# TensorE's order of matmul sets from a literal list in place of greedy rules, with 26 more score tiles on VectorE

## The chip, the core and the metric

The kernel runs on one NeuronCore of a Trainium2 chip. Times are device microseconds from start to end of one execution. Executions of one kernel mostly agree within 0.4%. In the profile PE is TensorE, PEld its weight loads, ACT ScalarE, DVE VectorE, POOL GpSimd.

## The reference

Two branches over the same input of 2048 rows of 512, mixed by a gate: attention with 32 heads of 16, and a gated MLP of width 1792.

```python
x = A_x
g = sigmoid((x * gate_w).sum(-1, keepdims=True))
a = softmax(q @ k.T * 16**-0.5) @ v ... @ wo          # 32 heads, 2048 x 2048 scores each
b = (sigmoid(x @ w_gate) * (x @ w_up)) @ w_down
return g * a + (1 - g) * b
```

The scores are the bulk: 32 units (8 groups of four heads by 4 chunks of 512 queries) of 64 tiles of 128 x 512, so 2048 tiles, each of which has to be exponentiated and multiplied with the values.

## The kernel before

The program is made by a scheduler that runs when the kernel is built. It holds tasks with assumed durations, walks through modelled time, and writes down an order for every engine. On the chip each engine plays its list, with semaphore waits where a task needs another engine's result or a buffer that another engine still uses. Nothing is chosen at run time.

A score tile goes one of two ways. Most ("R" tasks) are read from PSUM by ScalarE, two or three at a time, and written as exp into `PA`. Some ("RD") are read by VectorE, which forms exp from an integer conversion into a half-precision bit pattern and two shifted copies of it, so that such a tile needs three products with the values in place of one. How many go there is set by unit, in pairs:

```python
D_HALVES = (9, 9, 8, 8, 10, 6, 10, 9, 8, ...)     # pairs of tiles on VectorE, by unit

def make_exp(ts):                                  # ScalarE: 1, 2 or 3 tiles
    e = P.add("act", 0.175 + 0.3665 * len(ts), lambda a: a.activation(some(PA, out), some(ps_all, bs), ACTF.Exp, ...))
def make_x(ds):                                    # VectorE: conversion; two phase copies follow
    return P.add("dve", 0.076 + 0.534 * len(ds), lambda v: v.tensor_scalar(PDu[...], some(ps_all, bs), EXP_A, EXP_B, ...))
```

TensorE works in sets. A score set holds one to four score matmuls, each on its own quarter of the array's rows ("R" mode); a product set, or one step of a projection or of the MLP, holds four matmuls on quarters of the columns ("C" mode). All eight banks of PSUM, the memory that TensorE writes its results to, are shared by scores, products and projections; a bank is free again when another engine has read it. Which set comes next was decided by rules with some twenty thresholds, each with its own value by unit:

```python
def _pe(self, now):
    k = self.k = KNOBS[min(UNITS - 1, int(self.prog))]
    ...
    if p.nd == 0 and not late_d and nA + 2 <= k.N_A and ps.pick(2):      # scores possible?
        lead = self._lead(now)                                            # work queued on ScalarE
        ...                                                               # two or three tiles, VectorE's if due
        if lead < ((k.LATE_R if due and not ds else k.LATE) if len(s) >= 3 or whole else k.LATE_2) or (whole and lead < k.EARLY):
            return self._issue(s + ds, now, "R", [s + ds])
    ...                                                                   # VectorE's tiles that are behind
    low = ... sum(w for t, w in self.recent if t > now - WINDOW) < WARM
    if low and not hard: ... return self._fill(now)                       # a matmul with zero weights
    ...                                                                   # products, then projections and MLP
```

## Time and profile before

| | before |
|---|---|
| time, median | 748.98 us at first; 750.01 with the run beside the changed kernel |
| span in the profile | 747.7 us |
| busy: PE, ACT, DVE | 736.4, 718.3, 665.1 us |
| ScalarE: first exp, end of last exp | 13.6, 737.7 us |
| ScalarE's work between them, and what it loses | 699.6, 24.5 us |

Busy time is a poor guide: instructions overlap, so an exp that starts late within its predecessor's last 0.25 us leaves no idle time. I price each instruction at the median distance from its start to the next one's where the engine did not idle (0.904 us for an exp of two tiles, 1.330 for three, 0.477 for a tanh); "loss" is what is left of the stretch. (The prediction has 699.7 and 24.4, from a slightly different price for the small ones; its 13.0 of visible idle time includes 1.9 before the first exp.) The lines of the profile are in the prediction.

### The profile page before, as it was taken

How to read it: one execution, taken by the hardware profiler on the slowest of the kernel's cores; microseconds unless marked ns; L12 is line 12 of the kernel's file. 1: busy time of each engine (PE TensorE's matmuls, PEld its weight loads, DVE VectorE, ACT ScalarE, POOL GpSimd, SP SyncE). 2: the span in 40 equal slices, each digit the busy share in tenths (PEclk: the TensorE clock that was granted, in tenths of full speed). 3: DMA queues.
4: the chain of work that ended last, by engine and by line, in shares of the span. 5: the costliest groups of instructions: out<-in, count | busy, mean ns of one | idle time of the engine just before them, and what ended most of it. 6: DMA issues, size and time to landing. Idle time of an engine off the chain costs nothing.

```text
span 747.7 us, 22002 instructions
## 1 busy us (share of the span) xinstructions
PE 736.4 (98%) x9687; PEld 218.3 (29%) x9689; DVE 665.1 (89%) x1277; ACT 718.3 (96%) x790; POOL 149.5 (20%) x279
## 2 busy tenths in 40 slices
PE   9999999999999999999999999999999999999998
PEld 4332422322222222322222222222222222222232
DVE  3999999989988998889999999999996897899985
ACT  4899999999999999999999999999999999999995
POOL 5746456222011030011211000040112000000000
PEclk9999999999999999999999999999999999999999
DMA  8532111132010010101101000010101011000100
GB/s 165 163 85 44 24 23 23 44 79 38 9 23 15 16 37 11 21 15 23 23 16 24 8 23 16 22 37 16 17 16 22 16 23 23 9 9 9 16 2 30
DMA packets 59127, 23.17 MB, mean 31 GB/s; under 512 B 52000, under 2 KB 58008, under 8 KB 59032
## 3 DMA queue, kind: packets, MB, share of 16 engines
q1 hardware_dynamic: 57160, 21.11, 13.1%
q8 instruction: 76, 1.25, 0.7%
q10 hardware_dynamic: 1872, 0.66, 0.4%
q14 instruction: 19, 0.16, 0.1%
HBM read 7.60 MB, written 2.10 MB: 13 GB/s over the span
## 4 chain that ended last, share of the span: by engine, by line
ACT 56%; PE 39%; DVE 4%; SPq 1%; DMA 1%; issue 0%
ACT PA L1000 53%; PE ps_all L798 14%; PE ps_all L1046 13%; PE ps_all L1055 11%; ACT tT L984 3%; DVE PD L1016 1%; DVE PD L1011 1%; SPq L704 1%; DMA xT<-in_A_x_dram 1%; PE ps_all L942 1%; DVE am L859 0%; DVE un L846 0%; DVE V L956 0%; ACT un L832 0%; ACT V L954 0%
## 5 line engine op out<-in xcount | busy, mean ns | idle before, releaser
L1000 ACT ACTIVATE PA<-ps_all 128x1024 bf16<-128x1024 f32 (+1 forms) x720 | 698.8, 1181 | 13.0 <-PE ps_all L1046 8.1
L1016 DVE TENSOR_SCALAR PD<-ps_all 128x512 uint16<-128x512 f32 (+1 forms) x557 | 374.4, 690 | 49.5 <-PE ps_all L1046 40.1
L1046 PE MATMUL ps_all<-Q,K 32*128 32x512 bf16 x2032 | 303.1, 384 | 4.2 <-ACT PA L1000 2.6
L1055 PE MATMUL ps_all<-PA,V 128*17 128x512 bf16 x1486 | 229.0, 381 | 0.4 <-ACT PA L1000 0.2
L1011 DVE TENSOR_SCALAR PD<-PD 128x1024 uint16<-128x1024 uint16 (+1 forms) x490 | 219.6, 475 | 2.1
L1055 PE MATMUL ps_all<-PD,Vm 128*17 128x512 f16 x1124 | 178.9, 381 | 0.0
L1046 PEld LDWEIGHTS ps_all<-Q,K 32*128 32x128 bf16 x2032 | 76.3, 91 | 292.4 <-ACT PA L1000 249.4
L1055 PE MATMUL ps_all<-PD,V 128*17 128x512 f16 x562 | 134.3, 381 | 0.0
L1135 POOL TENSOR_TENSOR rs<-rec,e 128x16 f32<-128x16 f32 x32 | 8.5, 266 | 363.6 <-DVE rec L1133 363.6
L798 PE MATMUL ps_all<-xT,wg 128*32 128x512 bf16 x896 | 71.4, 384 | 0.0
L798 PE MATMUL ps_all<-un,hT 128*32 128x512 bf16 x896 | 70.5, 383 | 0.0
L798 PE MATMUL ps_all<-xT,wu 128*32 128x512 bf16 x896 | 69.1, 383 | 0.0
L1055 PEld LDWEIGHTS ps_all<-PA,V 128*17 128x17 bf16 x1486 | 53.8, 88 | 48.1 <-issue 36.6
L1055 PEld LDWEIGHTS ps_all<-PD,Vm 128*17 128x17 bf16 x1124 | 41.5, 88 | 38.1 <-issue 32.0
L987 DVE SCALAR_TENSOR_TENSOR hT<-tT,ps_all 128x512 bf16<-128x512 bf16 x56 | 38.1, 680 | 8.0 <-PE ps_all L798 7.1
L984 ACT ACTIVATE tT<-ps_all 128x512 bf16<-128x512 f32 x56 | 42.5, 763 | 0.0
L1055 PEld LDWEIGHTS ps_all<-PD,V 128*17 128x17 bf16 x562 | 31.5, 88 | 19.0 <-issue 14.9
L914 POOL COPY Q<-Q 128x512 bf16<-128x512 bf16 x15 | 9.9, 661 | 122.7 <-DVE Q L913 122.6
L817 POOL TENSOR_TENSOR mid<-mid 128x256 bf16<-128x256 bf16 (+3 forms) x60 | 28.4, 473 | 3.7
L798 PEld LDWEIGHTS ps_all<-xT,wu 128*32 128x32 bf16 x896 | 19.2, 95 | 26.8 <-issue 15.2
L798 PEld LDWEIGHTS ps_all<-un,hT 128*32 128x32 bf16 x896 | 18.6, 94 | 24.9 <-issue 17.6
L851 POOL TENSOR_SCALAR K<-un,msk 128x512 bf16<-128x512 bf16 x28 | 24.6, 886 | 2.5 <-ACT un L834 2.3
(106 smaller groups left out, 345.3 us busy)
## 6 DMA issues: line engine op xcount, KB each, us to landing
wg<-in_B_w_gate_dram SPq DMA_DIRECT2D x4, 448.0 KB
wu<-in_B_w_up_dram SPq DMA_DIRECT2D x4, 448.0 KB
un<-in_B_w_down_dram SPq DMA_DIRECT2D x7, 256.0 KB
out_dram<-ost SPq DMA_DIRECT2D x14, 128.0 KB
mid<-mid SPq DMA_TRANSPOSE x60
wo<-in_A_wo_dram SPq DMA_DIRECT2D x2, 256.0 KB
Q<-mid SPq DMA_DIRECT2D x30, 4.0 KB
un<-in_A_wqkv_dram SPq DMA_DIRECT2D x1, 384.0 KB
```

Source lines behind the costliest of these rows:

```text
L798: i = pe.matmul(bk(b)[32 * j:32 * j + 32, :], w()[:, 32 * j:32 * j + 32], x(), start=first, stop=last, tile_position=(0, 32 * j), skip_gro ...
L817: e = pl(0.22 + 0.054 * n, lambda g, n=n: g.tensor_tensor(v()[:, :, 0:n], v()[:, :, 0:n], v()[:, :, n:2 * n], ALU.add), [e], prio=0.5, buf ...
L851: eK[g, r, c] = P.add("pool", 1.0, lambda p, r=r: p.tensor_scalar(K[:, g, r, c * 512:(c + 1) * 512], kraw[:, kr.slot, :], msk[:, r:r + 1], ...
L914: cp = P.add("pool", 0.7, lambda p: p.tensor_copy(Q[:, bq.slot, 1, :], Q[:, bq.slot, 0, :]), [ev], [bq], kind="m")
L984: et = P.add("act", 0.48, lambda a: a.activation(tT[:, t_.slot, :], bk(b), ACTF.Tanh, scale=0.5), [l1], [b, t_], kind="m")
L987: e_h[c, ft] = P.add("dve", 0.62, lambda v: v.scalar_tensor_tensor(hT[:, h_.slot, :], tT[:, t_.slot, :], 1.0, bk(b2), ALU.add, ALU.mult), ...
L1000: e = P.add("act", 0.175 + 0.3665 * len(ts), lambda a: a.activation(some(PA, out), some(ps_all, bs), ACTF.Exp, bias=ACT_BIAS, scale=SCALE) ...
L1011: return v.tensor_scalar(a[:, :, x.n, :], a[:, :, 0, :], float(PH_OFF[x.n]), None, op0=ALU.add)
L1016: return P.add("dve", 0.076 + 0.534 * len(ds), lambda v: v.tensor_scalar(PDu[:, bp.slot, 0, i:i + len(ds), :], some(ps_all, bs), EXP_A, EX ...
L1046: return pe.matmul(bk(b), K[32 * j:32 * j + 32, g, r, kt * 128:(kt + 1) * 128], q, start=True, stop=True, tile_position=(32 * j, 0))
L1055: return pe.matmul(bk(bo_)[32 * j:32 * j + DH + 1, :], lhs(h), rhs(), start=t.first, stop=t.last, tile_position=(0, 32 * j), skip_group_ch ...
L1135: e2_ = P.add("pool", 0.2, lambda p: p.tensor_tensor(r4(rs), r4(rec), e2[:, 4 * c:4 * c + 4][:, :, None].to_broadcast([128, 4, 4]), ALU.mu ...
```

## The change

The intent: replace rules that decide one set at a time by a list found by search, have fewer and fuller score sets, and let VectorE take more of the exps. The scheduler still runs, but PE's part of it reads symbols: `R01.0` is a score set of the first two waiting ScalarE tiles and the first waiting VectorE tile, `C00123` a product set of all four lanes, `G`/`F` the start/next step of a projection or MLP group, `Z` a filler, `w2` "let two chances pass".

```diff
-D_HALVES = (9, 9, 8, 8, 10, 6, 10, 9, 8, 9, 10, 10, 7, ...)     # 562 tiles
+D_HALVES = (9, 9, 9, 9, 10, 7, 10, 10, 9, 10, 10, 10, 8, ...)   # 588 tiles
-LAT = {"pe": 0.25, ...}
+LAT = {"pe": 0.215, ...}
-KNOB_TABLE = dict(N_A=((5, 3), (6, 3), ...), ...)
+ORDER = ("0:F 1:C00123 2:R01.0 3:G 4:R01. 5:R01.1 ...",
+         "M333333333333333N00030003<0000000003000000300003030000000004400000300030=...",   # 2751 sets
+         "0 1 2 3 4 5 6 7 8 9 10 11 12 13 14 15 17 25 29 ...")                              # which group each G is
     def _pe(self, now):
-        k = self.k = KNOBS[min(UNITS - 1, int(self.prog))]
-        ...                                     # all rules
+        if self._next(now):
+            self.passed = 0
+            return True
+        self.passed += 1
+        return False
-        e = P.add("act", 0.175 + 0.3665 * len(ts), ...
+        e = P.add("act", 0.05 + 0.427 * len(ts), ...
-            x = P.add("dve", 0.36, ...
+            x = P.add("dve", 0.334, ...
```
(Cut: the rest of the list, the decoder, and some thirty assumed durations of this kind.)

## The prediction

> **What bounds the kernel now.** I read four views in this order: the page's busy shares and chain, the stretches by stage, the instruction groups by shape, and the chain in order of time. The page first:
>
> ```profile
> PE 736.4 (98%) x9687; PEld 218.3 (29%) x9689; DVE 665.1 (89%) x1277; ACT 718.3 (96%) x790; POOL 149.5 (20%) x279
> ...
> ACT 56%; PE 39%; DVE 4%; SPq 1%; DMA 1%; issue 0%
> ```
>
> Two engines look full, and the chain changes hands between them. ScalarE (ACT) computes exp of most score tiles, VectorE (DVE) of the rest. The stretches (us, then busy time of PE, weight loads, DVE, ACT, POOL) show that this is no average over unlike stages:
>
> ```profile
> 100.00:300.00 200.00, 198.33 (x2609) 56.97 (x2601) 182.43 (x342) 197.19 (x221) 47.98 (x81) 1.00 0.13 30
> 300.00:500.00 200.00, 198.13 (x2385) 54.76 (x2385) 186.93 (x357) 199.33 (x220) 26.94 (x50) 1.00 0.09 20
> 500.00:700.00 200.00, 199.55 (x2561) 55.67 (x2553) 176.64 (x340) 199.41 (x226) 18.50 (x36) 1.00 0.09 16
> ```
>
> For 600 us ACT idles 4 us and PE 4 us, at granted clock 1.00; DVE idles 54 us. Next, the costly groups by shape (count, then busy us and mean ns):
>
> ```profile
> L1000 ACT ACTIVATE PA<-ps_all 128x1024 bf16<-128x1024 f32 x674 | 640.2, 1159 | 6.2 <-PE ps_all L1055 3.4 <-PE ps_all L1046 2.5
> L1016 DVE TENSOR_SCALAR PD<-ps_all 128x512 uint16<-128x512 f32 x552 | 368.3, 685 | 49.4 <-PE ps_all L1046 40.1 <-PE ps_all L1055 4.9
> L1046 PE MATMUL ps_all<-Q,K 32*128 32x512 bf16 x2032 | 303.1, 384 | 4.2 <-ACT PA L1000 2.6
> L1011 DVE TENSOR_SCALAR PD<-PD 128x1024 uint16<-128x1024 uint16 x418 | 171.7, 434 | 2.1
> L1000 ACT ACTIVATE PA<-ps_all 128x1536 bf16<-128x1536 f32 x46 | 69.2, 1505 | 6.9 <-PE ps_all L1046 5.6 <-PE ps_all L1055 0.8
> ```
>
> The mean of an exp over two tiles, 1159 ns, is not its cost: consecutive ones overlap. The spacing is. The chain shows it, start, length, what:
>
> ```profile
> 400.99 38.51 ACT PA L1000 x42
> 439.50 0.05 issue
> 439.54 0.39 PE ps_all L1046 x2
> 439.93 0.32 PE ps_all L1055 x4
> 440.25 0.43 PE ps_all L798 x8
> 440.69 0.33 PE ps_all L1046 x4
> 441.01 0.54 PE ps_all L1055 x8
> ```
>
> 42 exps take 38.51 us, 0.917 each. Start-to-start over the whole trace, the median is 0.904 for two tiles (90th percentile 0.947), 1.330 for three, 0.477 for a tanh. Then the chain passes to PE, where a score set (L1046: up to four matmuls together, one per quarter of the rows) or a set of four column matmuls (L1055, L798) costs about 0.22 us, and 0.32 when the next set is of the other kind.
>
> **ACT's budget.** 674 x 0.904 + 46 x 1.330 + 56 x 0.477 + 2.5 (small ones) = 699.7 us. The first exp starts at 13.6, the last ends at 737.7, and 9.9 us of tail follow (last products, transposes, output projection, store). 747.7 - 13.6 - 9.9 = 724.1, so ACT loses **24.4 us**: 13.0 in the visible idle times, the rest in exps that start some 10 to 100 ns late but within their predecessor's overlap. By stage: about 7 us from 13.6 to 100, where projections crowd PE, 14 from 100 to 700, 3 after.
>
> **PE's budget.** From the first score at 13.2 us, grouping matmuls that start together, spacing is at its floor nearly everywhere: median 221 to 226 ns between sets of one kind, 321 and 322 across a change of kind. All time above the medians sums to **19.3 us**. DVE's instructions, priced at their back-to-back medians (0.601 per score tile, 0.335 per phase copy, 0.599 for two merged), sum to 632.7 us; DVE has room.
>
> **What the Trainium skill says.** "TensorEngine Tiling (Array Packing)", section Key Properties: "Changing tiling mode (not just tile) drains the TensorE". The trace agrees: 322 against 221 ns, some 100 ns a change, 1464 changes. "TensorE: Matmul & The Clock Gate", section Back-to-back issue gap, gives N/2.4 + 2.5 ns for a warm matmul, 216 ns at N = 512; same-kind spacing has its 10th percentile at 216. That figure is for one matmul; the trace shows one set of four in that time, so a half-empty set costs as much as a full one. "ScalarE: Activation LUTs", section What ACT_TABLE_LOAD costs, gives 0.833 ns per element plus 186 ns with immediates, less about 93 of overlap: 946 ns at 1024. The trace has 904, which I use. The clock page's section on HAM oscillation warns of a slower clock after idle windows of some 3.4 us; clock 1.00 throughout here, and that is what the filler matmuls are for.
>
> **The change part by part.** It keeps every operation but the split, and replaces the greedy rules, which chose TensorE's next set from a model when the program was built, by a literal list. The retuned durations affect only the planned order of the other engines and the waits. I decoded the list by counting its symbols, and counted the same in the kernel before's program:
>
> - Score sets: 843 before, 719 after, for the same 2048 tiles (2.43 and 2.85 to a set). Before: 260 sets of two ACT tiles alone and 124 of one DVE tile alone. After: 152 and 33; 538 are two ACT tiles with one DVE tile. That is -124 x 0.2165 = -26.8 us of PE.
> - Probability-times-value sets: 814 to 827. A tile moved to VectorE needs three products in place of one (52 more): +13 x 0.22 = +2.9.
> - Fillers: 10 to 2 (40 such matmuls show in the trace, in tens of sets of four): -8 x 0.22 = -1.7. Projections and MLP: unchanged, 1171.
> - Changes of kind after the first score: 1464 to 1428: -36 x 0.105 = -3.8.
>
> PE's sum: **-29.4 us**. With stalls as before PE alone would give 749.0 - 29.4 = 719.6; without its stalls, about 700.
>
> ACT: 1486 to 1460 tiles, in 692 twos, 25 threes and a single: 625.6 + 33.3 + 0.5 = 659.4 against 670.5: **-11.1 us**. On the path, since ACT sets the pace.
>
> DVE: 26 more tiles and 26 more phase copies: 15.6 + 8.7 = **+24.3 us**, to 657. Before, it would have lain in DVE's idle time.
>
> So after the change ACT is the highest floor: 13.6 + (699.7 - 11.1) + 9.9 = 712.1 us of span, 713.4 as timed (the timed median is 1.3 above the span). What remains is how much of the 24.4 us ACT still loses. Its losses come from scores that arrive late because PE was full: 97.4% of its time was set floors ((734.5 - 19.3)/734.5). At a time of 725 PE would be at 96.7%, so a little looser, and the order was searched for exactly these waits, with exp costs (0.904, 1.331) that equal the trace's medians where the old model had 0.908 and 1.275. Against it: DVE goes from 85 to 91%, and both share eight PSUM banks, so banks come free later. I take half: 12 us. Most of the early 7 stays, since the projections are the same; the gain is in the middle. 713.4 + 12 = **725 us**, -3.2%.
>
> **The rivals.** (1) ACT keeps its whole loss: only the moved tiles count, 749.0 - 11.1 = 738, same within 2%. For it: ACT is busy 99% from 100 on, and its visible idle time there is only 4 us. Against it: spacing above 0.904 is hidden in that busy time, and PE's 29 us come from the place that makes scores late. (2) PE's saving counts in full because PE was the true bound, with its stalls kept: 720. For it: PE's spacing is at its floor. It needs ACT's loss down to 6. (3) DVE becomes the bound: its 657 plus about 20 of start and end and the 50 us that it waits for scores now would give 727 or more; its waits shrink only if the list feeds it evenly. For: a mixed set every 1 us or so does that; against: pairs of DVE tiles and evictions for the MLP come in bursts. (4) The fixed list is right in the plan and wrong on the chip: TensorE stalls in order on a tile that is late, and nothing else fills. 740 to 750. For: PE had only 19 us of stalls. Against: the plan before was also fixed at build time and held to 98%, so this is no new kind of risk. (5) Fewer fillers let the clock fall: it would need microseconds of idle PE, and none is planned.
>
> **Range and chances.** The floor is 713; a loss of 3 to 23 us gives 716 to 736. Faster by over 2% is below 734.0, a loss below 20.6 us. The move of tiles itself speaks for a small loss: it costs PE 2.9 us and DVE 24, and pays only where ACT is already near its floor. Faster 0.87, within 2% 0.12, slower 0.01.
>
> **What would show it.** Exps over two tiles: 692, with median spacing still 0.904 and fewer above 0.92; ACT's loss, computed as here, near 12 instead of 24. Score sets 719, spacing across kinds still 0.32, and PE's time above the medians larger than 19 (near 30), as it now waits. DVE's busy time near 690 and its idle time before L1016's score tiles well below 49. Chain of waits: ACT's share above 56%, PE's below 39%. I would be wrong if ACT's spacing stays at 0.917 on the mean (rival 1), if weight loads or matmuls of scores wait much longer for DVE (rival 3), or if the clock drops below 1.00.

## The result, and the profile after

| | before | changed |
|---|---|---|
| time, median (4 runs each) | 750.01 us | 732.39 us |
| span in the profile | 747.7 | 730.2 |
| first exp starts | 13.6 | 12.3 |
| ScalarE's work from first to last exp | 699.6 | 688.4 |
| ScalarE's loss in it | 24.5 | 20.0 |
| of that, visible idle time | 11.2 | 7.4 |
| from the last exp to the end | 9.9 | 9.5 |

The ratio is 0.9763 (95% interval 0.9746 to 0.9781): faster, by 2.4%. Ratios are the mean time of one kernel's fast runs over that of the other's of the same rounds, so not quite the ratio of the medians quoted. The rows add up: -1.35 (start) - 11.2 (work) - 4.5 (loss) - 0.4 (tail) = -17.5, the whole difference of the spans. The start is partly chance: in traces with the same order of instructions it falls anywhere within about 1 us.

Busy shares and chain of the changed kernel:

```profile
PE 719.5 (99%) x9719; PEld 211.1 (29%) x9721; DVE 681.8 (93%) x1301; ACT 706.5 (97%) x788; POOL 153.2 (21%) x279
...
ACT 49%; PE 29%; DVE 21%; issue 0%
```

The stretches (us; busy time of PE, weight loads, DVE, ACT, POOL; clock; DMA share; GB/s):

```profile
100.00:300.00 200.00, 197.87 (x2741) 57.78 (x2741) 196.21 (x366) 194.63 (x216) 52.19 (x88) 1.00 0.15 31
300.00:500.00 200.00, 198.90 (x2574) 53.60 (x2574) 196.56 (x377) 199.81 (x227) 31.27 (x53) 1.00 0.10 20
500.00:700.00 200.00, 198.65 (x2557) 54.55 (x2559) 180.68 (x352) 200.00 (x227) 17.16 (x32) 1.00 0.08 16
```

Groups by shape (count, busy us, mean ns, idle time of the engine before them):

```profile
L949 ACT ACTIVATE PA<-ps_all 128x1024 bf16<-128x1024 f32 x692 | 658.1, 1169 | 7.0 <-PE ps_all L995 5.0 <-PE ps_all L1004 1.4
L965 DVE TENSOR_SCALAR PD<-ps_all 128x512 uint16<-128x512 f32 x586 | 389.5, 682 | 26.8 <-PE ps_all L995 23.8 <-PE ps_all L1004 1.2
L960 DVE TENSOR_SCALAR PD<-PD 128x1024 uint16<-128x1024 uint16 x380 | 159.2, 438 | 1.8
L960 DVE TENSOR_SCALAR PD<-PD 128x2048 uint16<-128x2048 uint16 x104 | 75.2, 734 | 0.0
L949 ACT ACTIVATE PA<-ps_all 128x1536 bf16<-128x1536 f32 x25 | 39.5, 1581 | 0.9 <-PE ps_all L995 0.9
```

Three things are to be seen. VectorE absorbed its 26 tiles out of idle time: the idle time before its score tiles fell from 49.4 to 26.8 us. It now stands in the chain with 21% where it had 4%. And from 100 to 300 us ScalarE is busy less than before (194.63 of 200 against 197.19): by the accounting above it loses 8.0 us between 100 and 200 (4.5 before), but 3.4 from 13.6 to 100 (7.0 before) and 6.4 from 200 to 700 (9.9 before). Instructions count in the stretch where they start, so each figure is good to about 1 us.

Counted in the built program, the changed kernel has 751 score sets, and the prediction's 719 is a wrong sum of its own: 718 sets hold an exp's tiles, 33 more hold a VectorE tile alone. Those 33 are named in the prediction and were left out of its total.

### The profile page after: what moved, and what is told of

Same layout as the page of the kernel before. It is cut to its first block, busy times and chain, and to the rows that moved or that the text cites. A ratio compares the mean times of both kernels' runs of the same rounds, so it can differ in the third digit from the quotient of the medians.

```text
span 730.2 us, 22086 instructions
## 1 busy us (share of the span) xinstructions
PE 719.5 (99%) x9719; PEld 211.1 (29%) x9721; DVE 681.8 (93%) x1301; ACT 706.5 (97%) x788; POOL 153.2 (21%) x279
## 4 chain that ended last, share of the span: by engine, by line
ACT 49%; PE 29%; DVE 21%; issue 0%
ACT PA L949 46%; DVE PD L965 11%; PE ps_all L995 10%; PE ps_all L747 9%; PE ps_all L1004 9%; DVE PD L960 7%; ACT tT L933 2%; PE ps_all L891 1%; DVE hT L936 1%; DVE mid L1064 1%; DVE un L795 1%; DVE am L808 1%; PE ps_all L730 0%; DVE Q L862 0%; PE ps_all L750 0%; DVE V L905 0%
## 5 line engine op out<-in xcount | busy, mean ns | idle before, releaser
L949 ACT ACTIVATE PA<-ps_all 128x1024 bf16<-128x1024 f32 (+1 forms) x718 | 687.4, 1183 | 7.9 <-PE ps_all L995 6.0
L965 DVE TENSOR_SCALAR PD<-ps_all 128x512 uint16<-128x512 f32 x587 | 390.7, 683 | 26.8 <-PE ps_all L995 23.8
L995 PE MATMUL ps_all<-Q,K 32*128 32x512 bf16 x2032 | 285.1, 384 | 2.4 <-ACT PA L949 1.4
L1004 PE MATMUL ps_all<-PA,V 128*17 128x512 bf16 x1460 | 241.1, 381 | 0.3 <-DVE hT L1060 0.2
L960 DVE TENSOR_SCALAR PD<-PD 128x1024 uint16<-128x1024 uint16 (+1 forms) x484 | 231.2, 502 | 1.8
L1004 PE MATMUL ps_all<-PD,Vm 128*17 128x512 f16 x1176 | 196.1, 381 | 1.0 <-DVE PD L960 0.9
L995 PEld LDWEIGHTS ps_all<-Q,K 32*128 32x128 bf16 x2032 | 71.4, 91 | 290.4 <-ACT PA L949 254.0
L1004 PE MATMUL ps_all<-PD,V 128*17 128x512 f16 x588 | 130.5, 381 | 1.1 <-DVE PD L965 0.8
L747 PE MATMUL ps_all<-xT,wg 128*32 128x512 bf16 x896 | 73.1, 384 | 0.2 <-DVE hT L936 0.2
L747 PE MATMUL ps_all<-un,hT 128*32 128x512 bf16 x896 | 73.1, 382 | 0.0
L747 PE MATMUL ps_all<-xT,wu 128*32 128x512 bf16 x896 | 70.3, 383 | 0.4 <-DVE PD L965 0.4
L1004 PEld LDWEIGHTS ps_all<-PD,Vm 128*17 128x17 bf16 x1176 | 45.4, 88 | 40.8 <-issue 30.8
L936 DVE SCALAR_TENSOR_TENSOR hT<-tT,ps_all 128x512 bf16<-128x512 bf16 x56 | 37.9, 677 | 1.3 <-PE ps_all L747 1.3
L747 PEld LDWEIGHTS ps_all<-xT,wu 128*32 128x32 bf16 x896 | 19.0, 95 | 28.0 <-issue 14.0
L747 PEld LDWEIGHTS ps_all<-un,hT 128*32 128x32 bf16 x896 | 19.6, 94 | 20.7 <-issue 14.0
```

Source lines behind the costliest of these rows:

```text
L747: i = pe.matmul(bk(b)[32 * j:32 * j + 32, :], w()[:, 32 * j:32 * j + 32], x(), start=first, stop=last, tile_position=(0, 32 * j), skip_gro ...
L936: e_h[c, ft] = P.add("dve", 0.597, lambda v: v.scalar_tensor_tensor(hT[:, h_.slot, :], tT[:, t_.slot, :], 1.0, bk(b2), ALU.add, ALU.mult), ...
L949: e = P.add("act", 0.05 + 0.427 * len(ts), lambda a: a.activation(some(PA, out), some(ps_all, bs), ACTF.Exp, bias=ACT_BIAS, scale=SCALE), ...
L960: return v.tensor_scalar(a[:, :, x.n, :], a[:, :, 0, :], float(PH_OFF[x.n]), None, op0=ALU.add)
L965: return P.add("dve", 0.064 + 0.534 * len(ds), lambda v: v.tensor_scalar(PDu[:, bp.slot, 0, i:i + len(ds), :], some(ps_all, bs), EXP_A, EX ...
L995: return pe.matmul(bk(b), K[32 * j:32 * j + 32, g, r, kt * 128:(kt + 1) * 128], q, start=True, stop=True, tile_position=(32 * j, 0))
```

## The experiments

Theory to test: ScalarE sets the pace in both kernels, and the gain is its 11 us of moved work plus less waiting for scores, because PE has fewer sets to issue. Rivals: PE's number of sets sets the pace; VectorE has become the bound; or the gain is in the order alone.

### One part of the change at a time

Three kernels keep the greedy rules and take over the split, the durations, or both. (With the durations comes one line of the scheduler, which sets from when on a set that changes the mode is counted in modelled time.)

```diff
 # b_split: the kernel before
-D_HALVES = (9, 9, 8, 8, 10, 6, 10, 9, ...)
+D_HALVES = (9, 9, 9, 9, 10, 7, 10, 10, ...)
 # b_const: the kernel before
-LAT = {"pe": 0.25, ...};  0.175 + 0.3665 * len(ts);  0.36; 0.48; 0.61; ...
+LAT = {"pe": 0.215, ...}; 0.05 + 0.427 * len(ts);    0.334; 0.477; 0.6; ...
 # b_both: the two together
```

> The kernel before with its greedy rules and only the new split, 588 in place of 562 tiles on VectorE. If ScalarE sets the pace and the moved tiles count by themselves: 750 - 11 = 739 us. If PE sets the pace: no gain or a loss, 750 to 755, since PE gets 13 more product sets (+2.9 us) and the rules form no fuller score sets. I expect about 748, as I think both are tight.

> The kernel before with only the retuned durations and latencies of the model (split and rules as before). If the gain were the better model: 740 or less. If the model's numbers matter only together with the searched list: 750 within 5 us either way, since knobs tuned for the old numbers now meet others.

> Everything of the change but the searched list: new split and retuned durations under the greedy rules. If the list is what makes the gain: 745 to 755. If the split makes it: 739 or less.

| | time | ratio to before | PE score sets | ScalarE work | ScalarE loss | last exp to end |
|---|---|---|---|---|---|---|
| before | 749.29 | | 843 | 699.6 | 24.5 | 9.9 |
| b_split | 764.59 | 1.0207 | 880 | 687.8 | 42.9 | 17.7 |
| b_const | 762.46 | 1.0166 | 790 | 699.6 | 37.7 | 9.7 |
| b_both | 760.92 | 1.0176 | 858 | 687.9 | 37.9 | 19.7 |
| changed | 732.39 | 0.9763 | 751 | 688.4 | 20.0 | 9.5 |

All three give the right result and all three are slower than the kernel before, by more than I expected. (By the 2% rule b_const counts as "same", the other two as "unclear"; but the intervals of all three ratios, 1.0126 at the lowest, lie above 1. The clock was 0.998 in the trace of b_const; a fifth of a per cent does not make 13 us.) Two readings follow. The split by itself takes its 11.8 us from ScalarE and gets none of it: the loss grows by 18.4 us and the tail by 7.8. The rules made 37 more score sets, not fewer, and TensorE had work left over when the last exp was done; that the sets are the cause is not shown. And b_const is the clean case against counting sets: it has 53 score sets **fewer** than the kernel before and the same ScalarE work, and it is 13 us slower. Its ScalarE waits longer for the right sets. Its busy shares, and its exps with their idle time (which was 6.2 us in the kernel before):

```profile
PE 737.1 (97%) x9709; PEld 217.9 (29%) x9709; DVE 669.8 (88%) x1282; ACT 720.3 (95%) x791; POOL 149.0 (20%) x279
```

```profile
L1000 ACT ACTIVATE PA<-ps_all 128x1024 bf16<-128x1024 f32 x677 | 640.3, 1152 | 13.6 <-PE ps_all L1055 6.6 <-PE ps_all L1046 6.6
L1046 PE MATMUL ps_all<-Q,K 32*128 32x512 bf16 x2032 | 295.5, 385 | 15.6 <-ACT PA L1000 12.1 <-DVE PD L1016 1.4 <-DVE am L859 0.3
```

PE idles 15.6 us before scores (4.2 before), for banks that ScalarE still reads, while ScalarE idles for scores. Both wait for each other in turn. On the chip b_const does the same work as the kernel before, but for a few fillers; only order and grouping differ, since the durations exist in the model alone. So its 13 us are a matter of order, of which part is not shown. The step from b_both to the changed kernel, 28.5 us, is the list's, together with the removal of the rules' shifts in when VectorE's tiles come due. What in the list earns it, the 107 sets fewer than in b_both or their places, is not separated. It does not follow that rules are worse as such: their thresholds had been tuned to the old durations and the old split, and these three kernels did not tune them again.

### Less work on one engine, with every order kept

These kernels shorten instructions of one engine by leaving out columns. The order of instructions and all semaphores stay as they are. The exps and VectorE's conversions then leave some columns stale, and the products leave some sums short, so the numbers are wrong; the two kernels with shortened products alone (b_pe, a_pe), and the one below that has them, failed the comparison with the reference, while the others happened to pass it, which shows that its tolerance is wide, not that they are right.

```diff
 # b_act, a_act: exps from the 91st on, 12 of 512 columns per tile left out
-a.activation(some(PA, out), some(ps_all, bs), ACTF.Exp, ...)
+a.activation(some(PA, out, 500), some(ps_all, bs, 500), ACTF.Exp, ...)
 # b_pe, a_pe: products, all but the first of each bank
-pe.matmul(bk(bo_)[32 * j:32 * j + DH + 1, :], lhs(h), rhs(), ...)
+pe.matmul(bk(bo_)[32 * j:32 * j + DH + 1, 0:472], lhs(h), rhs()[:, 0:472], ...)
 # b_dve: VectorE's conversions ("evictions" in the texts below) from the 41st on
-v.tensor_scalar(PDu[:, bp.slot, 0, i:i + len(ds), :], some(ps_all, bs), ...)
+v.tensor_scalar(PDu[:, bp.slot, 0, i:i + len(ds), 0:490], some(ps_all, bs, 490), ...)
```

> The kernel before, every exp from the 91st on shortened to 500 of 512 columns per tile (wrong result on purpose): takes some 13.0 us of work (1300 tiles x 12 columns x 0.833 ns by the spacing of 2 and 3 tiles) from ScalarE, with the order of everything kept. If ScalarE sets the pace: 9 us or more faster. If PE does: 3 us or less. Both tight: 4 to 8.

> The kernel before, every product matmul but the first of each bank over 472 of 512 columns (wrong result on purpose): takes some 13.0 us from PE (781 sets x 40 columns[...] of the measured 0.216 us for 512). If PE sets the pace: 9 us or more faster. If ScalarE does: 3 us or less. Both tight: 4 to 8.

> The kernel before, VectorE's score evictions from the 41st on over 490 of 512 columns (wrong result on purpose): takes some 12 us (522 x 22 columns at 1.04 ns, the slope of 0.601 and 1.134 us for one and two tiles) from VectorE. It has 80 us of idle time there, so: 0 to 2 us faster. If VectorE mattered before already: 4 or more.

> The changed kernel with the same cut of ScalarE, some 12.8 us of work. If after the change ScalarE alone is the bound: 9 us or more faster than 732. If PE or VectorE have become as tight: 3 to 6. If one of them is the bound: 0 to 2.

> The changed kernel with the same cut of PE, some 13.2 us of work. If the change relieved PE, as the prediction said: 4 us or less faster than 732. If PE is still the bound: 8 or more.

| | cut | time | ratio to before | ScalarE loss |
|---|---|---|---|---|
| before | | 749.91, 749.25 | | 24.5 |
| b_act | 12.9 us of ScalarE | 744.21 | 0.9922 | 32.6 |
| b_pe | about 13 us of PE | 747.79 | 0.9995 (0.9945 to 1.0046) | 23.4 |
| b_dve | about 12 us of VectorE | 748.80 | 0.9996 (0.9979 to 1.0012) | 24.4 |
| changed | | 732.39 | 0.9763 | 20.0 |
| a_act | 12.8 us of ScalarE | 726.92 | 0.9692 | 27.6 |
| a_pe | about 13 us of PE | 732.16 | 0.9762 | 19.7 |

The cuts are real: the exp of two shortened tiles follows its predecessor after 0.884 to 0.885 us instead of 0.904, a product set after 0.204 to 0.205 instead of 0.221. In both kernels PE's cut is worth nothing that the interval shows, VectorE's in the kernel before neither, and ScalarE's is worth 5 to 6 of 13 us. (Without the execution at a lower clock, b_pe's others, 747.35 to 748.01, lie some 2 us below all seven of the kernel before, 749.01 to 750.85. Of that, 0.9 is an earlier first exp, which is chance as far as known, and 1.1 is loss.) By the bands set beforehand, both cuts of PE fall in the lowest, so PE alone is not the bound; the cuts of ScalarE do not reach the 9 us named for ScalarE alone, and fall in the band for two tight engines. So ScalarE sets the pace, before and after, with something close behind it, and the belief that a full PE makes its loss is wrong in this form: with 13 us less to do, PE left ScalarE's loss at 23.4 and 19.7. Nor does PE's busy share show the cut; this is b_pe, beside 736.4 us and 98% in the kernel before:

```profile
PE 732.0 (98%) x9689; PEld 218.7 (29%) x9689; DVE 665.4 (89%) x1277; ACT 718.1 (96%) x790; POOL 149.7 (20%) x279
```

The weight loads of three consecutive score sets show how, at the same place of the list; in brackets is the idle time before each and what ended it. First the kernel before, then b_pe:

```profile
445.04 0.09 PEld L1046 LDWEIGHTS ps_all<-Q,K 32*128 32x128 bf16 x2 [0.25 <-ACT PA L1000]
...
445.96 0.09 PEld L1046 LDWEIGHTS ps_all<-Q,K 32*128 32x128 bf16 x2 [0.49 <-ACT PA L1000]
...
446.87 0.11 PEld L1046 LDWEIGHTS ps_all<-Q,K 32*128 32x128 bf16 x3 [0.48 <-ACT PA L1000]
```

```profile
443.62 0.09 PEld L1046 LDWEIGHTS ps_all<-Q,K 32*128 32x128 bf16 x2 [0.28 <-ACT PA L1000]
...
444.54 0.09 PEld L1046 LDWEIGHTS ps_all<-Q,K 32*128 32x128 bf16 x2 [0.48 <-ACT PA L1000]
...
445.46 0.11 PEld L1046 LDWEIGHTS ps_all<-Q,K 32*128 32x128 bf16 x3 [0.49 <-ACT PA L1000]
```

In both, the sets start 0.91 to 0.92 us apart, each released by an exp: that is the time of one exp of two tiles, not of what PE does in between. The products between them are shorter in b_pe, and the score sets wait for their banks all the same. In this stretch the chain of waits names PE at every step and PE's matmuls overlap into an unbroken row; yet its work does not set the length.

That only 5 to 6 of ScalarE's 13 us come through says that something else is close behind. The two joint cuts ask what, in the changed kernel; in the kernel before it was not asked, nor was VectorE's cut over the whole run tried alone in the changed kernel.

```diff
 # a_act_pe: the cuts of a_act and of a_pe;  a_act_dve: those of a_act and of b_dve
```

> The changed kernel with both cuts, 12.8 us of ScalarE and 13.2 of PE (wrong result on purpose). Alone they gave 5.5 and 0.2 us. If PE is the next bound right behind ScalarE: 10 or more faster than 732, about 721. If something else holds ScalarE's scores back (VectorE, or the trip of a bank from engine to engine): about 726, no more than ScalarE's cut alone.

> The changed kernel with the cut of ScalarE (12.8 us) and a cut of VectorE over all score evictions from the 41st on, 490 of 512 columns, some 12.5 us. If VectorE, 93% busy since the change, is the next bound: 10 or more faster than 732, about 721. If PE is: about 727 as with ScalarE's cut alone. 724 would say both share it.

a_act_pe took 723.70 us (ratio 0.9651, 0.9635 to 0.9667) and a_act_dve 724.74 (0.9663, 0.9648 to 0.9677), against 726.92 for ScalarE's cut alone. With ScalarE shorter, PE's 13 us are worth 3.2 and VectorE's 12.5 are worth 2.2, where PE's alone had been worth nothing. Both fall between what I had expected for "the next bound" and "not the next bound": the two share that place. Even so, 26 us of work taken from ScalarE and PE shortened the run by only 8.7; ScalarE's loss in that kernel is 24.1 us. What holds the rest I have not shown. The order of every engine is fixed in these kernels and was made for the uncut durations, which is one candidate; the untouched engine is another. The chain names it (VectorE with 49% in a_act_pe, PE with 67% in a_act_dve), which alone proves nothing, as the stretch at 445 us showed.

### Is VectorE the bound where ScalarE loses most?

Between 100 and 200 us VectorE is nearly always busy and the chain runs through it. The same 80-tile cut, once there and once late:

```diff
 # a_dve_mid: the changed kernel, conversions 55 to 134 (some 95 to 190 us);  a_dve_late: 470 to 549 (some 570 to 670 us)
-v.tensor_scalar(PDu[:, bp.slot, 0, i:i + len(ds), :], some(ps_all, bs), ...)
+v.tensor_scalar(PDu[:, bp.slot, 0, i:i + len(ds), 0:400], some(ps_all, bs, 400), ...)
```

> The changed kernel, the 80 score evictions of VectorE between 95 and 190 us over 400 of 512 columns: takes 80 x 0.117 = 9.3 us from VectorE in the stage where it is 95% full and ScalarE loses 8 us. If VectorE is the bound of this stage: 3 to 6 us faster. If ScalarE's loss there comes from the order of sets on PE: 0 to 1.

> The same cut, 80 evictions of 9.3 us in all, between 570 and 670 us, where VectorE has idle time and ScalarE loses 2 us in 100: 0 to 1 us faster if VectorE bounds only the stage from 100 to 200; 3 or more if VectorE's latency matters everywhere.

a_dve_mid took 731.54 us (ratio 0.9763, 0.9749 to 0.9778), a_dve_late 732.19 (0.9774, 0.9759 to 0.9789). Set against 732.39 that is 0.9 and 0.2 us, and by the ratios to the kernel before (0.9763 for the changed kernel) nothing. The stage itself, first of the changed kernel, then of a_dve_mid (busy PE, weight loads, DVE, ACT, POOL):

```profile
100.00:200.00 100.00, 98.00 (x1443) 31.00 (x1439) 99.49 (x178) 94.63 (x105) 39.21 (x64) 1.00 0.18 39
```

```profile
100.00:200.00 100.00, 98.34 (x1459) 30.83 (x1458) 95.36 (x179) 95.77 (x107) 39.39 (x64) 1.00 0.18 39
```

VectorE gained idle time, and ScalarE got 1 us of it. (The first exp of a_dve_mid started 0.9 us later than in the changed kernel, so its profiled span, 730.1 us against 730.2, hides this.) The waits of the stage (who waits for whom: us in total, times, longest), again changed kernel and a_dve_mid, show what did not move: ScalarE's longest wait is for a score set, 1.9 us both times.

```profile
ACT PA L949 <- PE ps_all L995: 4.1, 6, 1.9
```

```profile
ACT PA L949 <- PE ps_all L998: 3.1, 4, 1.9
```

The chain of the changed kernel ahead of that wait tells why:

```profile
148.12 0.39 PE ps_all L995 x3
148.51 0.32 PE ps_all L1004 x4
148.83 0.89 PE ps_all L891 x64
149.72 0.21 PE ps_all L1004 x4
149.94 0.86 PE ps_all L747 x16
150.80 0.65 PE ps_all L1004 x12
151.45 0.38 PE ps_all L995 x4
151.82 0.02 issue
151.85 0.26 DVE PD L965
```

From 148.5 to 151.4 the list has PE do a value projection (L891, 64 small matmuls), a query projection (L747) and products, and no score set. An exp of two tiles takes 0.9 us, so ScalarE runs dry and idles 1.9 us:

```profile
151.81 1.02 ACT L949 ACTIVATE PA<-ps_all 128x1024 bf16<-128x1024 f32 x1 [1.92 <-PE ps_all L995]
```

That is a choice of the list, and in a_dve_mid, with VectorE's conversions shorter, the same exp waits as long. For the largest of the stage's waits this theory holds by the trace; a list without this gap was not tried.

No kernel of these that computes the right result beats the changed one.

## Why the prediction was right or wrong

The direction, the class (faster by over 2%) and the range (716 to 736) held; the point, 725, was 7.4 us too low, and the gain of 24 (from 749.0) was in truth 17.6 (from 750.0).

- **"ACT is the highest floor": right.** Of the cuts made alone, only ScalarE's clearly shortens either kernel; but with 5 to 6 of 13 us, so the next floor is close.
- **ACT -11.1 us: right** in size; the trace has 11.2, and 692 exps of two tiles at an unchanged median of 0.904. But it is no gain that stands by itself: the split under the old rules took the same work away and cost 15 us.
- **"I take half: 12 us" of loss: the step that failed.** The loss went from 24.5 to 20.0. That is 8.0 us against the point. Unplanned gains at the start (1.35, luck) and the tail (0.4) gave some of it back; the timed runs lie 2.2 above the profiled span where 1.3 was assumed, and rounding took 0.4: together the 7.4. Its ground failed with it: "Its losses come from scores that arrive late because PE was full." Score sets are late, but taking 13 us from PE leaves the loss within about 1 us of where it was. For the largest wait the trace shows that what counts is when the list places the score set; for the rest of the loss the cause stays open. Of the loss, the part hidden in overlaps did not move at all: the exps of two tiles that follow without idle time have 8.3 us above the median in the kernel before and 8.8 after, where I had expected fewer above 0.92. Their mean spacing is 0.916 in both, close to the 0.917 that the prediction named as the sign of rival (1).
- **"Most of the early 7 stays; the gain is in the middle": half wrong.** The early loss halved (7.0 to 3.4), the middle lost 3.5 us less from 200 on and 3.5 more between 100 and 200.
- **PE -26.8 us for score sets: mis-sized.** The right count, 751, gives -92 x 0.2165 = -19.9. Changes of kind after the first score fell by 28, not 36, as a few early steps are not of the column kind: -2.9. PE's sum is then -19.9 + 2.9 - 1.7 - 2.9 = -21.6. With it PE would have been about 97.6% full at 725 (693.6 of 710.5 us), no "little looser" than the 97.4% before, so this ground for a smaller loss fell too. The time from the first score to the end fell by 16.1 (734.5 to 718.4), so PE waits some 5 us more. By the prediction's own tally of time above the medians, 19.3 became 19 to 20 where "near 30" was expected; that tally misses waits that split a set in two, since each piece is then counted as a set.
- **DVE +24.3 us: near.** At back-to-back prices its work rose by about 22, as 104 phase copies are merged (72 before); its busy time, overlaps taken out, by 16.7. The idle time before its score tiles, predicted well below 49, is 26.8.
- **Chain: ACT above 56% was wrong** (49%), PE below 39% right (29%). I did not foresee DVE's 21%, and that share turned out to mean little: taking 9.3 us from VectorE between 95 and 190 us gave 0.9 of run time at most.
- **The rivals.** (1), 738 with the loss unchanged, was nearer to the truth than I was, on the loss and in time (5.6 us off against 7.4). (2), PE as the bound, fell with b_pe and a_pe. (3), VectorE as the bound, fell for the stage that a_dve_mid cut; its time, 727 or more, was not excluded by the result. VectorE shares the second place with PE. (4), a list that does not hold on the chip, holds in small: the 1.9 us gap is of its kind, but planned rather than accidental. (5): the clock stayed at 1.000 with two fillers in place of ten.

## What to carry to other kernels

With three engines over 90% busy, busy shares and even the chain of waits did not say here which one to relieve. A test that does: shorten each engine's instructions a little, leaving the order alone, and see which cut comes through. Count the work of the pacing engine at start-to-start prices and treat what is left as its loss; ask of each piece of that loss which instruction stood in its place on the other engine. A shift of work between engines is only worth what the order lets through, so judge it together with an order made for it.

## What the Trainium skill lacked or had wrong

- "ScalarE: Activation LUTs", section What ACT_TABLE_LOAD costs: an estimate from its figures is at least 946 ns from one exp of 1024 columns to the next (186 + 0.833 x 1024, less 93 of overlap). The traces show 0.904 us, 1.330 at 1536 and 0.477 for a 512-column tanh, all from PSUM: 50 ns plus 0.833 ns per column. It is this page that is off for reads from PSUM; the skill as a whole is not without a figure that fits.
- "TensorEngine Tiling (Array Packing)", section Key Properties: it says that a change of mode drains, without a size. Here it is 322 against 221 ns, about 100 ns each, with little difference by what the score set holds (median to the next column set 0.304 us for one matmul, 0.321 for three, 0.325 for four).
- A warning not to take TensorE's busy share for its headroom is in the skill; no page has a measured case of work taken from it without effect on share or time. Here PE was 98% busy in the kernel before (736.4 us) and 98% busy in b_pe (732.0 us), which had 13 us less for it to do.
